# Sort matrices balanced on 128 rows of eight, row sums by ScalarE, column sums by TensorE, and the second half of them inside the first expert

## The chip, the cores and the metric

The kernel runs on one core of a Trainium2 chip. The metric is the time of one execution on the device, in microseconds (us). The core has five engines, each with its own list of instructions: TensorE (PE in the profile; its weight loads are PEld), VectorE (DVE), ScalarE (ACT), GpSimd (POOL) and SyncE (SP), which only issues DMAs here. They wait for one another by semaphores. GpSimd, SyncE and, for two transfers, ScalarE issue the DMAs.

## The reference

Four batches of eight heads, 768 positions of 64 numbers each. Every head has an 8x8 matrix `sort_net`, which is balanced in five rounds:

```
P = P - max over the row
P = exp(P)
P = P / (row sum + 1e-9)
P = P / (column sum + 1e-9)
```

The balanced matrix mixes the eight blocks of 96 positions of k and of v (`k_sorted[i] = sum over j of P[i, j] * k[j]`). Each block of q then attends to the sorted block of the same place: softmax of `q . k / 8`, times v. The result, 3072 rows of 512, is x of a mixture of eight experts. The gate's logits `x @ w_gate` are made an exponential and balanced in eight rounds of row and column normalization, and

```
out = sum over e of P[:, e] * (relu(x @ w1[e]) @ w2[e])
```

with w1 of 512x1024 and w2 of 1024x512.

## The kernel before

**The head.** `P`, the 32 matrices, lies on 32 partitions, one matrix of 64 numbers on each. Five rounds run on it: an exponent on ScalarE (line 415), and on VectorE the row sums, their reciprocal, the multiplication, the column sums, their reciprocal and the multiplication (lines 421 to 428). The row maximum is subtracted before the first round only (lines 410, 411). Between the rounds TensorE turns the queries of batch 0 (`wide_queries`, copied by ScalarE, line 286) and VectorE makes `mask16` (line 419).

**Spreading.** `P` is repeated 16 times along the columns (`Prep`, line 432, a part by VectorE and a part by ScalarE). `spread` then runs warm-up matmuls (`warm`: 128x512 products of zeros, whose result nobody reads) and eight small products with the identity `Ibig`, which put the matrices on 128 partitions, 16 for each column. `build_r` multiplies by `mask16` and makes `Rt`, the 128x128 sorting matrices of a batch. For batch 0 VectorE does it straight from the PSUM; for the others GpSimd does it from `Pb`, a copy of all 32 matrices that line 449 makes after a second `spread`.

**Batch 0.** `sort_pair` sorts v (line 273 copies to `vs`), `hop(0)` carries the values by eight DMAs from 128 partitions to the 96 of `vsb` (line 152), `wide_keys`, `wide_scores`, `wide_mix` and `turn` do the attention and leave x in `xtT`. A small copy on GpSimd, `gate` (line 451), waits for the hop; the loads of w1 of expert 0, of k and q of batch 1 and of w2 are issued behind it.

**First expert and batches 1 to 3.** From about 31 us on, expert 0 (`first_two`, steps of `hidden0`: four matmuls and one Relu on ScalarE, line 369; and of `output0`) is interleaved by hand with the attention of batches 1 to 3: `run(n)` takes n steps of the expert, `run_both` and `weave` alternate the two. `pin` (the name for `tc.keep_in_program_order`) holds an instruction at its place in the order written; the other instructions are placed by the framework. For batches 2 and 3, `queries` first rearranges q on GpSimd (`qr`, line 180). `build_r(2)` and `build_r(3)` stand behind the loads of their batches on GpSimd.

**Experts 1 to 7.** The gate's balancing (`balance`) runs beside the end of expert 0. It has a column sum by TensorE too: an f32 matrix of ones, 128x128, times the 128x8 partial sums `cs2` (line 607). After that, each expert is computed with seven products for eight blocks (`hidden`, line 623; `output7`, line 710), and VectorE adds the results to the output (`gather`, line 675).

Of the kernel before, what the change touches and what calls it, by code (L numbers as in the profile page):

```python
# [12 lines left out]

F32 = mybir.dt.float32
# [6 lines left out]
def mkap(t, dims, off=0):  # L21
    return bass.AP(tensor=t.tensor, offset=t.offset + off, ap=dims)
# [3 lines left out]
def kernel(  # L26
# [29 lines left out]
    sp = actx.enter_context(tc.tile_pool(name="sp", bufs=3))  # L56


    P = pp.tile([32, 8, 8], F32)
    nc.sync.dma_start(out=P, in_=sort_net.rearrange("b h i j -> (b h) i j"))  # L60

# [26 lines left out]

    load_batch(0, [("q", l0, 4) for l0 in (0, 4)])
    Ibig = ones.tile([128, 128], BF16)
    make_identity(nc, Ibig)
    load_batch(0, [(x, l0, 4) for x in "vk" for l0 in (0, 4)])
    wg = ones.tile([128, 4, E], BF16)
    pin(nc.gpsimd.dma_start(out=wg, in_=moe_w_gate.rearrange("(kk k) e -> k kk e", k=128)))
    load_batch(1, [("v", 0, 8)])
    blank = perp.tile([128, 512], BF16)
    nc.vector.memset(blank, 0.0)
    mask16 = ones.tile([128, 16], F32)  # L100


# [25 lines left out]
    Pb = perp.tile([128, 32, 8], F32)  # L128
    Rt = {}

    def build_r(bb, eng, n, pbps=None):

        Rt[bb] = perp.tile([128, 8, 8, 16], BF16, name=f"R{bb % 2}")
        for h in range(0, 8, n):
            ins = eng.tensor_tensor(
                out=mkap(Rt[bb], [Rt[bb].ap[0], [16, 8 * n], [1, 16]] if pbps is None else
                         [Rt[bb].ap[0], [128, n], [16, 8], [1, 16]], off=h * 128),
                in0=(mkap(Pb, [Pb.ap[0], [1, 8 * n], [0, 16]], off=(bb * 8 + h) * 8)
                     if pbps is None else
                     mkap(pbps, [pbps.ap[0], [1, n], [32, 8], [0, 16]], off=h)),  # L140
                in1=mkap(mask16, [mask16.ap[0], [0, 8 * n], [1, 16]] if pbps is None else
                         [mask16.ap[0], [0, n], [0, 8], [1, 16]]),
                op=ALU.mult)
            if eng is nc.gpsimd:
                pin(ins)


    def hop(bb):
        for i in range(NB):
# [15 lines left out]

    qT, kT, og = {}, {}, {}

    def queries(bb, hp, bank):

        qps = bank([128, 6, 128], BF16)  # L170
        if bb < 2:

            for kk in range(6):
                for h in range(2):
                    pin(nc.tensor.matmul(qps[64 * h:64 * h + 64, kk, :],
                                         qt[bb][:, 2 * hp + h, kk * 64:kk * 64 + 64],
                                         Ibig, is_transpose=True, start=True, stop=True))
        else:
            qr = sp.tile([128, 6, 2, 64], BF16, name="qr", bufs=2)
            nc.gpsimd.tensor_copy(  # L180
                qr.rearrange("p kk h d -> p h kk d"),
                qt[bb][:, 2 * hp:2 * hp + 2].rearrange("p h (kk d) -> p h kk d", d=64))
            for kk in range(6):
                pin(nc.tensor.matmul(qps[:, kk, :], qr[:, kk].rearrange("p h d -> p (h d)"),
                                     Ibig, is_transpose=True, start=True, stop=True))
        qT[bb, hp] = sp.tile([128, 128, 6], BF16, name="qTs", bufs=4)
        nc.scalar.copy(qT[bb, hp], qps.rearrange("p kk c -> p c kk"))
# [89 lines left out]
    def wide_queries(hp, pair):  # L277
        qT[0, hp] = sp.tile([128, 128, 6], BF16, name="qTs", bufs=4)
        t = pair()
        for kk in range(6):  # L280
            for h in range(2):
                c = (kk % 3) * 128
                pin(nc.tensor.matmul(t[64 * h:64 * h + 64, kk // 3, c:c + 128],
                                     qt[0][:, 2 * hp + h, kk * 64:kk * 64 + 64], Ibig,
                                     start=True, stop=True))
        pin(nc.scalar.copy(
            qT[0, hp].rearrange("p x (b j) -> p x b j", b=2),
            t[:, :, 0:384].rearrange("p b (j x) -> p x b j", j=3)))

# [29 lines left out]

    def warm(t, n):  # L320
        for _ in range(n):
            pin(nc.tensor.matmul(t[:, 0, :], Ibig, blank, start=True, stop=True))

    def wide_mix(hp, pair):
        og[0, hp] = sp.tile([128, NB, 2, 64], BF16, name="og", bufs=2)
# [66 lines left out]
    def sum_w(e):  # L392
        wct[e] = (wcq if e % 2 == 0 else wcp).tile([128, 3, 2, F // 2], BF16, name="wc")
        for kk in range(2):
# [3 lines left out]
            for a, b, o, c in ((a21, a22, ALU.add, s1), (s1, a11, ALU.subtract, s2),  # L398
                               (a11, a21, ALU.subtract, a21), (a12, s2, ALU.subtract, s4)):
                pin(nc.gpsimd.tensor_tensor(out=c, in0=a, in1=b, op=o))  # L400
                yield

    with tc.tile_pool(name="ps0", bufs=4, space=bass.MemoryType.PSUM,
                      reuse_waits="tile") as ps0:
        pair = lambda: ps0.tile([128, 2, 512], F32, name="pair")
        warm(pair(), 4)
        rs = pp.tile([32, 8], F32)
        cs = pp.tile([32, 8], F32)
        Pt = P.rearrange("p i j -> p j i")
        nc.vector.reduce_max(out=rs, in_=P, axis=AX.X)  # L410
        nc.vector.tensor_sub(P, P, mkap(rs, [rs.ap[0], rs.ap[1], [0, 8]]))
        for it in range(5):


            pin(nc.scalar.activation(out=P, in_=P, func=AF.Exp))
            for hp in {2: (0, 1), 3: (2,), 4: (3,)}.get(it, ()):
                wide_queries(hp, pair)
            if it == 1:
                pin(nc.vector.reduce_sum(out=mask16, in_=Ibig.rearrange("p (j c) -> p c j", c=16),
                                         axis=AX.X))  # L420
            pin(nc.vector.reduce_sum(out=rs, in_=P, axis=AX.X))
            nc.vector.reciprocal(out=rs, in_=rs)
            nc.vector.tensor_mul(P, P, mkap(rs, [rs.ap[0], rs.ap[1], [0, 8]]))
            nc.vector.reduce_sum(out=cs, in_=Pt, axis=AX.X)
            if it == 0:
                nc.vector.tensor_scalar_add(cs, cs, 1e-9)
            nc.vector.reciprocal(out=cs, in_=cs)
            nc.vector.tensor_mul(Pt, Pt, mkap(cs, [cs.ap[0], cs.ap[1], [0, 8]]))

        Prep = perp.tile([32, 8, 8, 16], BF16, name="R1")  # L430
        for eng, i0, n in ((nc.vector.tensor_copy, 0, 5), (nc.scalar.copy, 5, 3)):
            eng(Prep[:, i0:i0 + n], mkap(P, [P.ap[0], [8, n], [1, 8], [0, 16]], off=i0 * 8))

        def spread(n):
            t = pair()
            warm(t, n)
            pbps = t[:, 0, 0:256].rearrange("p (i g) -> p i g", i=8)
            for i in range(8):
                pin(nc.tensor.matmul(pbps[:, i, :], Prep[:, i].rearrange("p j c -> p (j c)"),
                                     Ibig[0:32, 0:32], start=True, stop=True))  # L440
            return pbps

        build_r(0, nc.vector, 2, spread(7))
# [27 lines left out]
        hop(1)  # L471
# [10 lines left out]
    with ExitStack() as c2:  # L482
# [40 lines left out]
        for bb, ns in ((2, (5, 3, 2, 4)), (3, (5, 4, 0, 5))):  # L523
            at1 = attention(bb, bank1, usual)
            weave(at1, ex, 5, ns[0])
            if bb + 1 < B:
                load_batch(bb + 1, [(x, 0, 8) for x in "vkq"])
                build_r(bb + 1, nc.gpsimd, 4)
# [4 lines left out]
            if bb + 1 < B:  # L533
                weave(sort_values(bb + 1, bank1), ex, 5, ns[2])
# [318 lines left out]
```

## Time and profile before

| | |
|---|---|
| median of three runs | 678.27 us (676.98 to 680.12) |
| the profiled execution | 677.81 us |
| its span in the trace | 675.7 us |
| TensorE busy | 658.8 us, 98% |
| VectorE busy | 542.3 us, 80% |
| GpSimd busy | 469.5 us, 69% |
| ScalarE busy | 297.4 us, 44% |
| matrices on the chip | 2.48 us |
| balancing and spreading | 2.48 to 13.2 us |
| hop of batch 0 issued | 16.46 us |
| first step of expert 0 | 31.25 us |

A line of the timeline has the start and the duration in us, the engine, the line of the code, the operation, what is written and read with sizes, and how many such instructions were merged; in brackets stands how long the engine had been idle before and what ended that. A line of the busy times by stretch has the stretch, its length, the busy time and number of instructions of TensorE, of its weight loads, VectorE, ScalarE and GpSimd, the granted clock of TensorE as a share of the full one, the busy share of the DMA engines and the GB/s. In the first 13 us the trace has no record of the clock and shows 1.00; there, the matmuls of 512 columns of the warm-up start 0.43 us apart.

### The profile page before, as it was taken

How to read it: one execution, taken by the hardware profiler on the slowest of the kernel's cores; microseconds unless marked ns; L12 is line 12 of the kernel's file. 1: busy time of each engine (PE TensorE's matmuls, PEld its weight loads, DVE VectorE, ACT ScalarE, POOL GpSimd, SP SyncE). 2: the span in 40 equal slices, each digit the busy share in tenths (PEclk: the TensorE clock that was granted, in tenths of full speed). 3: DMA queues.
4: the chain of work that ended last, by engine and by line, in shares of the span. 5: the costliest groups of instructions: out<-in, count | busy, mean ns of one | idle time of the engine just before them, and what ended most of it. 6: DMA issues, size and time to landing. Idle time of an engine off the chain costs nothing.

```text
span 675.7 us, 13246 instructions
## 1 busy us (share of the span) xinstructions
PE 658.8 (98%) x5127; PEld 435.1 (64%) x5127; DVE 542.3 (80%) x1133; ACT 297.4 (44%) x536; POOL 469.5 (69%) x494
## 2 busy tenths in 40 slices
PE   6899999999999999999999999999999999999996
PEld 3666666554666666666666666666666666666675
DVE  7527768673798888888898888888898888888896
ACT  4673863469434343333434343333434343333430
POOL 4702435007987998898997898689886999636745
PEclk9799999999999999999999999999999999999999
DMA  9996964002140340031303040034003120001223
GB/s 158 184 217 110 162 115 61 3 1 31 33 63 1 63 64 1 1 64 13 52 1 58 6 63 1 3 62 63 1 1 65 22 42 1 0 1 64 95 79 141
DMA packets 32735, 36.57 MB, mean 54 GB/s; under 512 B 2016, under 2 KB 25792, under 8 KB 32672
## 3 DMA queue, kind: packets, MB, share of 16 engines
q0 software_dynamic: 26672, 27.32, 25.7%
q1 hardware_dynamic: 5776, 8.20, 3.8%
q8 instruction: 40, 0.66, 0.4%
q10 hardware_dynamic: 224, 0.20, 0.1%
q14 instruction: 23, 0.19, 0.1%
HBM read 52.45 MB, written 6.29 MB: 87 GB/s over the span
## 4 chain that ended last, share of the span: by engine, by line
PE 72%; DVE 1%; POOL 1%; issue 0%; ACT 0%; DVEq 0%
PE oacc L710 36%; PE bk L623 35%; PE bk L710 1%; DVE osbl L675 1%; POOL hs L693 1%; DVE hT L659 0%; DVE hT L662 0%; ACT p L643 0%; DVEq L675 0%
## 5 line engine op out<-in xcount | busy, mean ns | idle before, releaser
L675 DVE SCALAR_TENSOR_TENSOR osbl<-oacc,glog,osbl 128x256 f32<-128x256 f32 (+1 forms) x490 | 255.5, 522 | 61.6 <-PE oacc L710 61.4
L623 PE MATMUL bk<-xtT,w1e 128*128 128x512 bf16 x504 | 149.8, 379 | 0.0
L693 POOL TENSOR_TENSOR hs<-hT 128x512 bf16<-128x512 bf16 (+2 forms) x105 | 99.3, 959 | 68.1 <-DVE hT L662 68.0
L710 PEld LDWEIGHTS <-hT 128*128 128x128 bf16 x1008 | 98.4, 98 | 64.6 <-issue 1.1
L710 PEld LDWEIGHTS <-hs 128*128 128x128 bf16 x1008 | 98.4, 98 | 64.7 <-POOL hs L693 1.5
L710 PE MATMUL oacc<-w2e,hT 128*128 128x256 bf16 x796 | 119.6, 273 | 0.5 <-ACT hT L665 0.5
L665 ACT ACTIVATE hT<-bk 128x512 bf16<-128x512 f32 x84 | 50.3, 598 | 158.6 <-PE bk L623 158.6
L693 POOL TENSOR_TENSOR hs<-hT,hs 128x512 bf16<-128x512 bf16 (+2 forms) x105 | 99.9, 959 | 4.9
L693 POOL TENSOR_TENSOR hs<-hs,hT 128x512 bf16<-128x512 bf16 (+2 forms) x105 | 99.9, 959 | 4.3 <-ACT hT L665 0.4
L623 PE MATMUL bk<-xc,wc 128*128 128x512 bf16 x336 | 100.0, 379 | 0.2 <-ACT p L643 0.2
L710 PE MATMUL oacc<-w2e,hs 128*128 128x256 bf16 x612 | 92.0, 273 | 0.9 <-POOL hs L693 0.9
L651 ACT COPY u<-bk 128x512 f32<-128x512 f32 x84 | 49.2, 586 | 95.2 <-PE bk L623 94.4
L623 PEld LDWEIGHTS <-w1e 128*128 128x128 bf16 x672 | 65.6, 98 | 10.5
L659 DVE CUSTOM_DVE_ANT_0 hT<-bk,p 128x512 bf16<-128x512 f32 x84 | 58.1, 692 | 11.5 <-ACT p L656 6.4
L669 DVE SCALAR_TENSOR_TENSOR h<-bk,hT 128x512 bf16<-128x512 f32 x84 | 57.2, 680 | 5.7 <-ACT hT L665 5.7
L656 ACT COPY p<-bk 128x512 f32<-128x512 f32 x84 | 49.2, 586 | 23.5 <-PE bk L623 23.5
L643 ACT COPY p<-bk 128x512 f32<-128x512 f32 x84 | 49.3, 587 | 20.1 <-PE bk L623 20.1
L647 DVE CUSTOM_DVE_ANT_0 hT<-bk,p 128x512 bf16<-128x512 f32 x84 | 57.2, 680 | 1.0 <-ACT hT L369 0.6
L662 DVE CUSTOM_DVE_ANT_0 hT<-bk,u 128x512 bf16<-128x512 f32 x84 | 57.1, 680 | 1.0 <-PE bk L623 1.0
L710 PE MATMUL oacc<-w2s,hs 128*128 128x256 bf16 x364 | 54.8, 273 | 0.1
L623 PEld LDWEIGHTS <-wc 128*128 128x128 bf16 x504 | 49.2, 98 | 8.0 <-issue 0.4
L623 PE MATMUL bk<-xtT,wc 128*128 128x512 bf16 x168 | 50.0, 379 | 0.0
(138 smaller groups left out, 831.5 us busy)
## 6 DMA issues: line engine op xcount, KB each, us to landing
w2e<-in_moe_w_dram POOLq DMA_DIRECT2D x8, 1024.0 KB, 8.9
w1e<-in_moe_w_dram POOLq DMA_DIRECT2D x7, 1024.0 KB, 8.3
out_dram<-osbl SPq DMA_DIRECT2D x23, 256.0 KB, 2.0
kvq<-in_v_dram POOLq DMA_DIRECT2D x3, 768.0 KB, 14.1
kvq<-in_k_dram POOLq DMA_DIRECT2D x3, 768.0 KB, 13.5
vsb<-vs SPq DMA_DIRECT2D x19, 97.5 KB, 5.4
kvq<-in_q_dram POOLq DMA_DIRECT2D x4, 384.0 KB, 10.8
kvq<-in_q_dram POOLq DMA_DIRECT2D x2, 768.0 KB, 21.8
```

Source lines behind the costliest of these rows:

```text
L623: hold(nc.tensor.matmul(ps, wa[:, kk, :], xa[:, kk, :], start=(first and kk == 0), stop=(kk == 1), skip_group_check=True))
L643: nc.scalar.copy(p1, u)
L647: nc.vector._custom_dve(TENSOR_ADD_SAT, out=c11, in0=w, in1=p1, s0=TOP, s1=0.0)
L651: nc.scalar.copy(u2, u)
L656: nc.scalar.copy(p5, v)
L659: nc.vector._custom_dve(TENSOR_ADD_SAT, out=c22, in0=u, in1=p5, s0=TOP, s1=0.0)
L662: nc.vector._custom_dve(TENSOR_ADD_SAT, out=c12, in0=v, in1=u2, s0=TOP, s1=0.0)
L665: nc.scalar.activation(out=c21, in_=u, func=AF.Relu)
L669: nc.vector.scalar_tensor_tensor(out=h3[e, p][:, i, :], in0=u, scalar=0.0, in1=c22, op0=ALU.max, op1=ALU.subtract)
L675: nc.vector.scalar_tensor_tensor(out=o, in0=ps, scalar=glog[:, t, e:e + 1], in1=o, op0=ALU.mult, op1=ALU.add)
L693: nc.gpsimd.tensor_tensor(out=c, in0=a, in1=b, op=o)
L710: nc.tensor.matmul(ps, h[:, fb, :], w[:, fb, :], start=(first and fb == 0), stop=(fb == 3), skip_group_check=True)
```

## The change

`P` becomes 128 partitions of 2x8. Partition `64 * b + 8 * h + i` holds row i of head h, in the first eight numbers that of batch b and in the second eight that of batch 2 + b (b = 0, 1). Each half is balanced by `row_steps`: the exponent on ScalarE gives the row sum out as well (`accum_out`); VectorE takes its reciprocal and scales the row; TensorE multiplies by `same`, a matrix with ones where two partitions belong to the same head, which gives every partition its head's column sums; VectorE takes their reciprocal and multiplies. The maximum enters the first exponent as a bias.

The half of batches 0 and 1 runs in the head. Warm-up matmuls (now with `blank` as weights as well) and the query products of batch 0 stand between the column sums; two of the four ScalarE copies of query products follow the last two exponents, the other two follow the spreading. One copy (`rep`) and one product (`spread`) put the half on the partitions where `build_r` needs it. `Pb` gets batch 1 from the same product.

The half of batches 2 and 3 is advanced by `run`: after every second step of the first expert one more round, then the spreading, then the copy to `Pb`.

`same` and `Ibig` are made on GpSimd by three selects, which in the built order all stand ahead of the loads of v and k; the fills before them are VectorE's. The query rearrangement for batches 2 and 3 (`turned`) is pinned behind `build_r` for the first two pairs of heads.

```diff
-    P = pp.tile([32, 8, 8], F32)
-    nc.sync.dma_start(out=P, in_=sort_net.rearrange("b h i j -> (b h) i j"))
+    P = pp.tile([128, 2, 8], F32)
+    nc.sync.dma_start(out=P, in_=sort_net.rearrange("(t b) h i j -> (b h i) t j", t=2))
...
-    make_identity(nc, Ibig)
-    load_batch(0, [(x, l0, 4) for x in "vk" for l0 in (0, 4)])
+    blank = perp.tile([128, 512], BF16)
+    nc.vector.memset(blank, 0.0)
+    same = perp.tile([128, 16, 8], F32)
+    nc.vector.memset(same, 1.0)
+    nc.vector.memset(Ibig, 0.0)
+    for pattern, base, step in (([[-8, 16], [0, 8]], 0, 1), ([[8, 16], [0, 8]], 7, -1)):
+        pin(nc.gpsimd.affine_select(out=same, in_=same, compare_op=ALU.is_ge, fill=0.0, base=base,
+                                    pattern=pattern, channel_multiplier=step))
+    load_batch(0, [("v", l0, 4) for l0 in (0, 4)])
+    pin(nc.gpsimd.affine_select(out=Ibig, in_=Ibig, compare_op=ALU.not_equal, fill=1.0, base=0,
+                                pattern=[[-1, 128]], channel_multiplier=1))
+    load_batch(0, [("k", l0, 4) for l0 in (0, 4)])
...
+    def turned(bb, hp):
+        qr[bb, hp] = sp.tile([128, 6, 2, 64], BF16, name="qr", bufs=2)
+        pin(nc.gpsimd.tensor_copy(
+            qr[bb, hp].rearrange("p kk h d -> p h kk d"),
+            qt[bb][:, 2 * hp:2 * hp + 2].rearrange("p h (kk d) -> p h kk d", d=64)))
...
     def warm(t, n):
         for _ in range(n):
-            pin(nc.tensor.matmul(t[:, 0, :], Ibig, blank, start=True, stop=True))
+            pin(nc.tensor.matmul(t[:, 1, :], blank[:, 0:128], blank, start=True, stop=True))
...
+    def row_steps(g, ps):
+        W = P[:, g]
+        rs = pp.tile([128, 1], F32, name="rs")
+        cs = pp.tile([128, 8], F32, name="cs")
+        top = pp.tile([128, 1], F32, name="top")
+        pin(nc.vector.reduce_max(out=top, in_=W, axis=AX.X, negate=True))
+        for it in range(5):
+            pin(nc.scalar.activation(out=W, in_=W, func=AF.Exp, accum_out=rs,
+                                     bias=top if it == 0 else 0.0))
+            yield 5
+            nc.vector.reciprocal(out=rs, in_=rs)
+            nc.vector.tensor_scalar(out=W, in0=W, scalar1=rs, scalar2=None, op0=ALU.mult)
+            c = ps[:, 8 * it:8 * it + 8]
+            pin(nc.tensor.matmul(c, same.rearrange("p g i -> p (g i)"), W, start=True, stop=True))
+            yield it
+            if it == 0:
+                nc.vector.tensor_scalar_add(cs, c, 1e-9)
+            nc.vector.reciprocal(out=cs, in_=cs if it == 0 else c)
+            nc.vector.tensor_mul(W, W, cs)
+
+    def spread(g, ps):
+        rep = perp.tile([128, 8, 16], BF16, name="rep")
+        nc.vector.tensor_copy(rep, mkap(P, [P.ap[0], [1, 8], [0, 16]], off=8 * g))
+        pin(nc.tensor.matmul(ps, rep.rearrange("p j c -> p (j c)"), Ibig, start=True, stop=True))
...
-        warm(pair(), 4)
...
+        ct = pair()
+        warm(ct, 5)
+        copies = []
+        for it in row_steps(0, ct[:, 0, 0:40]):
+            if it < 5:
+                if it == 2:
+                    pin(nc.vector.reduce_sum(
+                        out=mask16, in_=Ibig.rearrange("p (j c) -> p c j", c=16), axis=AX.X))
+                if it > 1:
+                    copies.append(wide_queries(it - 2, pair))
+                if it < 4:
+                    warm(ct, (2, 3, 1, 1)[it])
+            elif copies:
+                copies.pop(0)()
+        t = pair()
+        spread(0, t[:, 0, 0:128])
+        copies.append(wide_queries(3, pair))
+        for copy in copies:
+            copy()
+        build_r(0, nc.vector, 2, t[:, 0, 0:128])
+        nc.vector.tensor_copy(Pb[:, 8:16].rearrange("p g i -> p (g i)"), t[:, 0, 64:128])
...
-        nc.vector.tensor_copy(Pb, spread(0).rearrange("p i g -> p g i"))
-        build_r(1, nc.gpsimd, 4)
+        build_r(1, nc.gpsimd, 4, Pb)
...
+        count = [0]
+
+        def rows():
+            for _ in row_steps(1, bank1([128, 40], F32)):
+                if _ < 5:
+                    yield
+            ps = bank1([128, 128], F32)
+            spread(1, ps)
+            yield
+            nc.vector.tensor_copy(Pb[:, 16:32].rearrange("p g i -> p (g i)"), ps)
+            yield
+
+        later = rows()
+
         def run(n):
             for _ in range(n):
                 next(ex)
+                count[0] += 1
+                if count[0] % 2 == 0:
+                    next(later, 0)
...
-        build_r(2, nc.gpsimd, 4)
+        build_r(2, nc.gpsimd, 4, Pb)
+        for hp in range(2):
+            turned(2, hp)
```

More of the change, by code (lines that the diff above doesn't have):

```diff
@@ L10 @@
 from concourse.dve_ops import TENSOR_ADD_SAT
-from concourse.masks import make_identity
 from concourse._compat import with_exitstack
@@ L97 @@
     load_batch(1, [("v", 0, 8)])
-    blank = perp.tile([128, 512], BF16)
-    nc.vector.memset(blank, 0.0)
     mask16 = ones.tile([128, 16], F32)
@@ L129, with build_r @@
     Rt = {}
-    def build_r(bb, eng, n, pbps=None):
+    def build_r(bb, eng, n, src):
         Rt[bb] = perp.tile([128, 8, 8, 16], BF16, name=f"R{bb % 2}")
@@ L135, in build_r @@
             ins = eng.tensor_tensor(
[L136 to L142, printed above, removed]
+                out=mkap(Rt[bb], [Rt[bb].ap[0], [16, 8 * n], [1, 16]], off=h * 128),
+                in0=mkap(src, [src.ap[0], [1, 8 * n], [0, 16]], off=(bb * 8 + h) * 8),
+                in1=mkap(mask16, [mask16.ap[0], [0, 8 * n], [1, 16]]),
                 op=ALU.mult)
@@ L166 @@
     qT, kT, og = {}, {}, {}
+    qr = {}
+    def turned(bb, hp):
[3 more added lines that the diff above has]
+            qt[bb][:, 2 * hp:2 * hp + 2].rearrange("p h (kk d) -> p h kk d", d=64)))
     def queries(bb, hp, bank):
@@ L178, in queries @@
         else:
[L179 to L182, printed above, removed]
+            if (bb, hp) not in qr:
+                turned(bb, hp)
             for kk in range(6):
-                pin(nc.tensor.matmul(qps[:, kk, :], qr[:, kk].rearrange("p h d -> p (h d)"),
+                pin(nc.tensor.matmul(qps[:, kk, :], qr[bb, hp][:, kk].rearrange("p h d -> p (h d)"),
                                      Ibig, is_transpose=True, start=True, stop=True))
@@ L285, in wide_queries @@
                                      start=True, stop=True))
-        pin(nc.scalar.copy(
+        return lambda: pin(nc.scalar.copy(
             qT[0, hp].rearrange("p x (b j) -> p x b j", b=2),
@@ L405 @@
         pair = lambda: ps0.tile([128, 2, 512], F32, name="pair")
-        warm(pair(), 4)
[L407 to L441, printed above, removed]
@@ L443 @@
-        build_r(0, nc.vector, 2, spread(7))
+        ct = pair()
[12 more added lines that the diff above has]
+                copies.pop(0)()
@@ L527 @@
                 load_batch(bb + 1, [(x, 0, 8) for x in "vkq"])
-                build_r(bb + 1, nc.gpsimd, 4)
+                build_r(bb + 1, nc.gpsimd, 4, Pb)
             else:
@@ L533 @@
             if bb + 1 < B:
+                for hp in range(2):
+                    turned(bb + 1, hp)
                 weave(sort_values(bb + 1, bank1), ex, 5, ns[2])
```

## The prediction

> **What bounds the kernel now.** I read the page's busy shares first, then the busy time by stretch, then the timeline of the first 17 us and of the first expert, and last TensorE's waits.
>
> ```profile
> PE 658.8 (98%) x5127; PEld 435.1 (64%) x5127; DVE 542.3 (80%) x1133; ACT 297.4 (44%) x536; POOL 469.5 (69%) x494
> ```
>
> TensorE is the bound over the span. The stretches (duration, PE busy, PE weight load, DVE, ACT, POOL, then the granted clock) say where it is not:
>
> ```profile
> 9.70:12.20 2.50, 2.50 (x8) 0.86 (x7) 1.94 (x9) 1.19 (x3) 0.00 (x0) 1.00 1.31 203
> 19.78:23.19 3.41, 3.17 (x45) 2.24 (x40) 0.96 (x1) 3.23 (x6) 1.71 (x3) 0.50 0.75 197
> 26.60:30.02 3.42, 2.85 (x49) 2.39 (x48) 3.15 (x10) 2.38 (x4) 3.42 (x5) 1.00 1.24 205
> 31.00:60.00 29.00, 28.79 (x350) 17.74 (x348) 12.54 (x39) 16.88 (x37) 2.10 (x4) 0.96 1.18 197
> ```
>
> Up to 31 us a chain through all engines sets the pace (the seven matmuls at 9.7 are warm-up work). From 31 us TensorE has 0.21 us idle in 29: whatever stops it there is paid in full, whatever ScalarE and VectorE do beside it is free. The head's chain, one round of the balancing:
>
> ```profile
> 0.74 1.28 ACT L415 ACT_TABLE_LOAD   x1 [0.74 <-PEq L837]
> ...
> 2.48 0.21 DVE L410 TENSOR_REDUCE rs<-P 32x8 f32<-32x64 f32 x1 [1.13 <-DMA P<-in_sort_net_dram]
> ...
> 2.97 0.26 ACT L415 ACTIVATE P<-P 32x64 f32<-32x64 f32 x1 [0.95 <-DVE P L411]
> ...
> 4.98 0.26 ACT L415 ACTIVATE P<-P 32x64 f32<-32x64 f32 x1 [1.75 <-DVE P L428]
> 5.26 0.21 DVE L421 TENSOR_REDUCE rs<-P 32x8 f32<-32x64 f32 x1
> 5.51 0.19 DVE L422 RECIPROCAL rs<-rs 32x8 f32<-32x8 f32 x1
> 5.73 0.21 DVE L423 TENSOR_TENSOR P<-P,rs 32x64 f32<-32x64 f32 x1
> 5.98 0.25 DVE L424 TENSOR_REDUCE cs<-P 32x8 f32<-32x64 f32 x1
> 6.27 0.19 DVE L427 RECIPROCAL cs<-cs 32x8 f32<-32x8 f32 x1
> ...
> 6.79 0.26 ACT L415 ACTIVATE P<-P 32x64 f32<-32x64 f32 x1 [1.55 <-DVE P L428]
> ```
>
> A round is 6.79 - 4.98 = 1.81 us. The first exponent starts at 2.97 and the copy behind the last round at 12.24. Then the first expert, where the second half of the balancing is put:
>
> ```profile
> 37.03 0.49 ACT L369 ACTIVATE hTs<-bank 128x384 bf16<-128x384 f32 x1 [0.16 <-PE bank L367]
> 37.68 0.49 ACT L369 ACTIVATE hTs<-bank 128x384 bf16<-128x384 f32 x1 [0.16 <-PE bank L367]
> ```
>
> One hidden step of TensorE takes 0.65 us; its Relu needs that step's last matmul. And the nearest likeness to the new column sum, which is f32, 128x128 on 128x8 too:
>
> ```profile
> 119.42 0.50 DVE L604 TENSOR_REDUCE cs<-glog 128x8 f32<-128x192 f32 x1
> ...
> 119.97 0.39 PE L607 MATMUL bk<-cs,onesc 128*128 128x8 f32 x2 [0.47 <-DVE cs L604]
> ...
> 120.39 0.17 DVE L608 TENSOR_SCALAR cs<-bk 128x8 f32<-128x8 f32 x1 [0.48 <-PE bk L607]
> ```
>
> VectorE to TensorE takes 0.05, TensorE to VectorE 0.42. The next hidden matmul follows at 120.21, so such a product takes 0.24 us of TensorE.
>
> **The change part by part: the head.** *Landing.* The matrices come as 256 rows of 32 B, not 32 of 256 B. Before, they landed 1.7 us after issue; the 128-row stores of the output take 2.0. I take +0.2 (0 to +0.6).
>
> *First exponent.* In the built kernel ScalarE's table load stands behind a wait for that landing, because the exponent now reads the loaded tile itself. The load (1.28) ran from 0.74, hidden; now it starts at 2.48 + 0.2 and the exponent at 4.0, not 2.97: +1.0. The maximum (0.21) lies beside it, and the dropped subtraction gains nothing. The trace shows only that an exponent ran 0.95 us after a load's end, so more than 0.95 behind a load is excluded. The Trainium skill, page "ScalarE: Activation LUTs", section "What ACT_TABLE_LOAD costs", gives 1283 ns and a drain of 1380, 2.66 us; by it the sum would be 1.4 larger, but the row allows no such drain behind the load.
>
> *Rounds.* Exponent to reciprocal: 0.28 in the rows less 0.05 for 56 fewer elements, plus 0.1 for giving out the row sum (no row has one; between 0 and 0.25, another ScalarE operation): 0.33. Reciprocal 0.22. Scaling 0.16 + 0.05 to TensorE = 0.21. Product to VectorE: 0.42 at full clock; at half clock up to 0.65; taken 0.5. Reciprocal 0.22, multiplication 0.20. Sum 1.68 against 1.81; over five rounds -0.6 (1.55 to 1.85: -1.3 to +0.2). The two to three warm-up matmuls (0.43 each at half clock) or twelve query products (0.75) ahead of each column sum fit inside a round.
>
> *Spreading.* From the last round's end to R's first part was 1.0 (two copies of 0.5, eight products). Now one 128x128 copy (0.2) and one product (0.4): -0.4. On VectorE a Pb copy (0.17) now stands before the value copies that release the hop: +0.17. The second spread and its 0.41 us copy at 17.21 go, where key copies cover them: 0 (to -0.4). GpSimd's two extra selects (0.3 each) delay the v loads' issue, which queue behind q loads that land until 8.2: 0.
>
> *Clock.* Fewer warm-up matmuls before 12.9, so the sorting may run at half clock: taken +0.3 (0 to +1). **Head: 1.0 - 0.6 - 0.4 + 0.17 + 0.3 = +0.5** (-1.3 to +2.2), passed on by hop, mix and turn.
>
> **The first expert.** Each round's column sum stands in TensorE's order after every second hidden step, and in ScalarE's order its exponent stands behind the Relus of both steps. Neither engine passes a waiting instruction (GpSimd sat 26.9 us at L180 until 59.1, with four hop DMAs behind it). So TensorE ends step two, and only then come: Relu 0.20 later, 0.49 long; exponent to reciprocal 0.33; reciprocal 0.22; scaling 0.21. That is 1.45 us of standing still, less up to 0.1 for the overlap of two ScalarE operations, plus 0.24 for the product: 1.6 a round. Nothing else can fill it: logits and the next hidden steps are behind the column sum in that queue. Five rounds: **8.0** (1.35 to 1.85: 6.8 to 9.2). The spread's copy stands on VectorE behind four key copies of 0.53 which need steps just before it: 0.7 of waiting and 0.1 of product, **+0.8** (0.2 to 1.0). The row maximum, Pb copy (0.2) and tensor operations lie beside TensorE: 0. R of batch 2 now waits for this Pb until some 52 us and takes 2.1; the q copies behind it wait for their load until 59.1 anyway: 0. These pinned q copies keep their place on GpSimd: 0; if a load came later than R, the hop DMAs behind them would wait as they do now. SP's queue keeps its order.
>
> Can the loss come back later? TensorE's waits from 31 to 165 us sum to 2.3 us, none on a DMA, so no.
>
> **Sum**: 0.5 + 8.0 + 0.8 = +9.3. The profiled execution took 677.81 with a span of 675.7; so 687.1. The median shown, 678.27, is 0.46 above it: **687.5 us**.
>
> **Rivals.** *The clock falls in the new gaps.* In the fourth stretch a clock of 0.96 over 29 us is half clock for its first 2.4 us, after a stretch whose idle gaps were under 1 us. With TensorE at work only 1.3 of 2.9 us, the same can happen here; a pair of hidden steps at half clock takes 1.3 more. Two such pairs: +2.6, 690.1 us. For it: two half-clock stretches already; against: these products fill the whole array, those of mix and turn 96 rows. The Trainium skill, "TensorE: Matmul & The Clock Gate", section "Why this matters for your kernels", asks for idle gaps above about 3 us before the clock drops; by that this rival adds nothing. The trace contradicts it, with a drop after gaps of at most 0.92 us, so it keeps its chance.
>
> *The exponent isn't held.* If ScalarE reached the exponent before the second Relu, a round (1.68) would run beside two hidden steps (1.30): 0.4 a round, 2.0, with the spread at 0.3 and the head at 0.5: 681.1, not slower by our measure. It decides where a round's cost falls under 0.5 us. Against it: the built order and one queue.
>
> *The head does what its shorter operations allow.* Row sums free and TensorE at full clock: the rounds gain 1.3, clock loss 0, landing 0: head -1.6, with the same stops: 685.4. For it: operations of 8 elements; against: the late table load.
>
> **Chances.** Forecast 0.66, own range 684 to 690; clock 0.14; exponent not held 0.10; fast head 0.10. The range reaches from 683.5 (short rounds and a fast head) to 691.5 (clock). A change within 0.5%, 3.4 us, is about what a measurement can't tell from none. Only the second rival ends within it: same 0.09, faster 0.01, slower 0.90.
>
> **What would show it.** The table load after 2.6 us and the first exponent near 4.0; rounds of 1.6 to 1.8 us; R's first part at 13.3 to 14. In the first expert five stops of TensorE of about 1.4 us, put down to VectorE's scaling, and the same five exponents on ScalarE straight behind a Relu; TensorE's idle time there about 8 us up. Stops under 0.5 us would make the prediction wrong, as would a delay that comes back before 165 us, where expert 1 begins.

## The result and the profile after

The changed kernel takes 697.17 us (median of six executions, 693.93 to 698.36); the kernel before, run beside it and earlier, takes 680.39 (six, 676.98 to 680.90). The ratio is 1.0264 [1.0243, 1.0285]: slower, as forecast, but by 16.8 us in the medians where the sum said 9.3, and outside the range of 684 to 690. The profiled execution took 697.36 us with a span of 695.2, against 677.81 and 675.7: 19.5 more. The working below goes by these two traces, since the forecast's sum was made against the first of them.

The stations of the two traces, in us from the start of the span (R stands for `Rt` of batch 0, the sorting matrices that `build_r` makes):

| | before | after | later by |
|---|---|---|---|
| first exponent | 2.97 | 4.00 | 1.0 |
| first part of R | 13.20 | 19.18 | 6.0 |
| first hop issued | 16.46 | 23.68 | 7.2 |
| first hidden step of expert 0 | 31.25 | 37.97 | 6.7 |
| first product of its output | 49.91 | 68.81 | 18.9 |
| end | 675.7 | 695.2 | 19.5 |

So the head costs 6.7 (forecast 0.5) and the part of the first expert up to its first output 12.2 (forecast 8.8); after that, 0.6 more is lost, from a cause that stays open, and nothing comes back.

The page of after, part 1, engines over the span:

```profile
PE 664.2 (96%) x5059; PEld 439.1 (63%) x5134; DVE 543.9 (78%) x1148; ACT 298.4 (43%) x550; POOL 469.9 (68%) x495
```

By the page TensorE is busy 5.4 us longer than before, and the span is 19.5 longer. The 5.4 is too low: behind the first output product both kernels run the same products, but this trace has 4521 matmul records there, with 614.0 us of busy time, and the trace of before 4596, with 617.5. Even with these 3.5 us added, more than half of the loss is TensorE standing still. Now the timeline of the head of after, the counterpart of the one round shown for before:

```profile
2.66 0.16 DVE L416 TENSOR_REDUCE top<-P 128x1 f32<-128x8 f32 x1 [1.01 <-DMA P<-in_sort_net_dram]
2.70 1.28 ACT L418 ACT_TABLE_LOAD   x1 [2.70 <-DMA P<-in_sort_net_dram]
...
4.00 0.30 ACT L418 ACTIVATE P<-P,top 128x8 f32<-128x8 f32 x1
4.21 0.18 ACT L418 ACTIVATION_READ_ACCUMULATOR P<-P,top 128x1 f32 x1
...
7.06 0.21 ACT L418 ACTIVATE P<-P 128x8 f32<-128x8 f32 x1 [2.67 <-DVE P L429]
...
7.88 0.60 PE L424 MATMUL pair<-P,same 128*128 128x8 f32 x2 [1.50 <-DVE P L422]
8.33 1.44 PE L330 MATMUL pair<-blank 128*128 128x512 bf16 x3
9.81 0.21 DVE L428 RECIPROCAL cs<-pair 128x8 f32<-128x8 f32 x1 [1.98 <-PE pair L330]
...
10.25 0.21 ACT L418 ACTIVATE P<-P 128x8 f32<-128x8 f32 x1 [2.89 <-DVE P L429]
...
17.49 0.60 PE L424 MATMUL pair<-P,same 128*128 128x8 f32 x2 [1.30 <-DVE P L422]
18.13 0.21 DVE L428 RECIPROCAL cs<-pair 128x8 f32<-128x8 f32 x1 [0.69 <-PE pair L424]
```

The table load now starts when the matrices have landed, and the exponent follows it at 4.00. A round then takes 10.25 - 7.06 = 3.19 us. The reason stands in the bracket of the line at 9.81: the reciprocal of the column sums is released by line 330, the warm-up matmuls, and not by line 424, the column sum. In the fifth round, which has no warm-up work behind its column sum, the same reciprocal is released by line 424, 0.64 after the product's start, and the round takes 1.89. VectorE's waits from 4 to 19 us (total, times, longest):

```profile
DVE cs L428 <- PE pair L330: 5.7, 3, 2.0
...
DVE cs L427 <- PE pair L330: 1.6, 1, 1.6
```

The warm-up matmuls write the second half of the PSUM tile `ct`, whose first half holds the column sums. By these rows the reader is made to wait for the last product that writes the tile; the first experiment tests that.

The stage of the first expert, from its first hidden step to its first output product (columns as in the table of stretches shown for before), first of after, with the part of it that ran at half clock, then of before:

```profile
37.97:68.81 30.84, 24.06 (x246) 13.21 (x244) 9.25 (x34) 13.55 (x37) 3.65 (x4) 0.80 1.06 178
...
43.57:53.81 10.24, 7.34 (x24) 3.09 (x22) 1.54 (x8) 3.19 (x11) 0.00 (x0) 0.50 1.26 217
```

```profile
31.25:49.91 18.66, 18.45 (x235) 11.14 (x233) 4.99 (x10) 12.53 (x27) 0.95 (x1) 0.94 1.26 217
```

TensorE's idle time in this stage goes from 0.21 to 6.78 us, and its busy time from 18.45 to 24.06. In that time the clock was granted at half from 43.57 to 53.81, three windows of 3.41 us running. One of the stops, in the timeline of after, and TensorE's waits from 37 to 69 us:

```profile
44.61 0.49 ACT L377 ACTIVATE hTs<-bank 128x384 bf16<-128x384 f32 x1 [0.59 <-PE bank L375]
45.00 0.20 ACT L418 ACTIVATE P<-P 128x8 f32<-128x8 f32 x1
45.09 0.19 ACT L418 ACTIVATION_READ_ACCUMULATOR P<-P 128x1 f32 x1
45.32 0.16 DVE L421 RECIPROCAL rs<-rs 128x1 f32<-128x1 f32 x1 [2.17 <-ACT P L418]
45.52 0.23 DVE L422 TENSOR_SCALAR P<-P,rs 128x8 f32<-128x8 f32 x1
45.80 0.60 PE L424 MATMUL bank<-P,same 128*128 128x8 f32 x2 [1.23 <-DVE P L422]
46.25 2.72 PE L375 MATMUL bank<-xtT,w1e 128*128 128x384 bf16 x8
```

```profile
PE bank L424 <- DVE P L422: 6.3, 5, 1.3
...
PE bank L434 <- DVE rep L433: 0.3, 1, 0.3
```

Relu, exponent, reciprocal, scaling, column sum: the chain of the forecast, five times, with 6.3 us of waiting. Behind it, two hidden steps take 2.72 us; at full clock they take 1.46.

### The profile page after: what moved, and what is told of

Same layout as the page of the kernel before. It is cut to its first block, busy times and chain, and to the rows that moved or that the text cites. A ratio compares the mean times of both kernels' runs of the same rounds, so it can differ in the third digit from the quotient of the medians.

```text
span 695.2 us, 13216 instructions
## 1 busy us (share of the span) xinstructions
PE 664.2 (96%) x5059; PEld 439.1 (63%) x5134; DVE 543.9 (78%) x1148; ACT 298.4 (43%) x550; POOL 469.9 (68%) x495
## 4 chain that ended last, share of the span: by engine, by line
PE 66%; POOL 3%; DMA 1%; DVE 1%; issue 1%; ACT 0%; DVEq 0%
PE oacc L745 34%; PE bk L658 31%; POOL hs L728 2%; DMA w1e<-in_moe_w_dram 1%; POOL wc L408 1%; PE bk L745 1%; DVE osbl L710 1%; POOL w2e L87 0%; POOL w1e L408 0%; DVE hT L694 0%; DVE hT L697 0%; ACT p L678 0%; DVEq L710 0%
## 5 line engine op out<-in xcount | busy, mean ns | idle before, releaser
L658 PE MATMUL bk<-xtT,w1e 128*128 128x512 bf16 x475 | 143.5, 379 | 0.9
L658 PE MATMUL bk<-xc,wc 128*128 128x512 bf16 x319 | 96.3, 379 | 0.6 <-ACT p L678 0.2
L658 PE MATMUL bk<-xc,w1e 128*128 128x512 bf16 x159 | 48.0, 379 | 0.0
## 6 DMA issues: line engine op xcount, KB each, us to landing
kvq<-in_k_dram POOLq DMA_DIRECT2D x3, 768.0 KB, 12.5
```

What stands on the lines that cost most here:

```text
L658: hold(nc.tensor.matmul(ps, wa[:, kk, :], xa[:, kk, :], start=(first and kk == 0), stop=(kk == 1), skip_group_check=True))
```

## The experiments

A median alone separates little here: an execution's time goes with the granted clock that it happened to get (below), so the stations in the traces carry the separate readings, and the medians the sum. All ratios are to the kernel before, run beside it. The runs from "own tile" to "rounds issued ahead" shared one chip, the next three a second, the last two a third; across these groups ratios are compared, not medians.

| run | median us | ratio, 95% |
|---|---|---|
| after | 697.17 | 1.0264 [1.0243, 1.0285] |
| own tile | 694.09 | 1.0235 [1.0184, 1.0286] |
| filled stops | 693.73 | 1.0219 [1.0184, 1.0254] |
| early table load | 693.82 | 1.0227 [1.0178, 1.0277] |
| rounds issued ahead | 684.87 | 1.0091 [1.0063, 1.0120] |
| own tile and ahead | 684.94 | 1.0074 [1.0048, 1.0100] |
| no waits | 681.76 | 1.0024 [1.0003, 1.0044] |
| no waits, more warm-up early | 680.87 | 1.0012 [0.9995, 1.0029] |
| the same, warm-up late as well | 681.92 | 1.0038 [1.0023, 1.0053] |
| all matrices in the head | 681.46 | 1.0041 [1.0017, 1.0065] |

**The warm-up matmuls get a PSUM tile of their own.**

```diff
+        wt = pair()
         ct = pair()
-        warm(ct, 5)
+        warm(wt, 5)
...
-                    warm(ct, (2, 3, 1, 1)[it])
+                    warm(wt, (2, 3, 1, 1)[it])
```

> The head's warm-up matmuls write a PSUM tile of their own; their number and places stay. Theory A: the reciprocal of the column sums waits for the last matmul that writes the same tile, which is a warm-up matmul. Then rounds 1 to 4 fall from 3.2 us to the 1.9 us of the fifth, expert 0 starts some 5 us earlier (near 33 us, from 38.0) and the time is 692 us. Rival B: the f32 product itself ends late at half clock, or its result is only told once the matmuls behind it are through. Then the rounds stay at 3.2 us and the time at 697.

In the timeline of this kernel the reciprocal is released by the column sum while the warm-up still runs:

```profile
7.10 0.60 PE L424 MATMUL pair<-P,same 128*128 128x8 f32 x2 [0.76 <-DVE P L422]
7.55 1.44 PE L330 MATMUL pair<-blank 128*128 128x512 bf16 x3
7.73 0.21 DVE L428 RECIPROCAL cs<-pair 128x8 f32<-128x8 f32 x1 [0.69 <-PE pair L424]
...
14.48 1.42 DVE L142 TENSOR_TENSOR R<-pair,mask 128x256 bf16<-128x256 f32 x4 [0.38 <-PE pair L434]
```

The later rounds fall to 1.9 to 2.0 us and R's first part comes 4.70 earlier, at 14.48. That the shared tile is the cause of the long rounds is shown. The first hidden step gains only 3.18 (34.79), because the way from the hop to it takes 15.81 us and not 14.29; of that way 3.5 ran at half clock here, 1.2 in after. The median gains 3.1, but the two intervals overlap.

**The stops filled with work.** Five products of zeros into a bank of their own are put ahead of each column sum in the first expert: TensorE's order and the chain stay, but it no longer stands idle.

```diff
         def rows():
+            fill = bank1([128, 512], F32)
             for _ in row_steps(1, bank1([128, 40], F32)):
-                if _ < 5:
+                if _ == 5:
+                    for _ in range(5):
+                        pin(nc.tensor.matmul(fill, blank[:, 0:128], blank, start=True, stop=True))
+                else:
                     yield
```

> In the first expert five 128x512 products of zeros, 0.22 us each at full clock and 0.43 at half, are put ahead of each of the five column sums, into a bank of their own, so that TensorE works while it would stand still. Theory A: about 5 us of the 12 lost in that stage come from the clock, which the gaps bring down to a half for three stretches of 3.4 us. Then the clock stays up there, a pair of hidden steps takes 1.3 us and not 2.7, and the time falls by 3 to 5 us, to 693. Rival B: the stops alone cost it. Then the time stays at 697 or rises by up to 2.

The stage in this kernel, and one stop in its timeline:

```profile
37.89:65.59 27.70, 26.45 (x272) 14.62 (x269) 9.24 (x34) 13.57 (x37) 2.50 (x3) 0.95 1.18 197
```

```profile
44.11 1.24 PE L523 MATMUL bank<-blank 128*128 128x512 bf16 x5
...
45.50 0.39 PE L424 MATMUL bank<-P,same 128*128 128x8 f32 x2 [0.15 <-DVE P L422]
45.75 1.46 PE L375 MATMUL bank<-xtT,w1e 128*128 128x384 bf16 x8
```

The filling and the rest of the wait take 1.39 us, where the stop had taken 1.23, so no useful work is gained. The half clock is down to one window, 37.41 to 40.82, the hidden steps behind the column sum take 1.46 again, and the stage is 3.14 shorter than in after. It is 9.04 longer than in the kernel before, which is what the stops, the products and the spread cost at full clock. The clock's share of the stage is thus 3.1 us of 12.2, shown by giving TensorE work that does nothing. The other executions agree: the granted clock was 0.995 to 0.998 in the four of this kernel, 0.986 to 0.996 in the six of after. The kernels that kept the stops empty had the long stretch of half clock each time: 39.60 to 53.25 with the own tile, 43.02 to 53.26 with the early table load.

**The rounds issued ahead.** The exponent, reciprocal and scaling of a round are issued three hidden steps before its column sum; batch 2's R is built one step later, to fit.

```diff
             nc.vector.tensor_scalar(out=W, in0=W, scalar1=rs, scalar2=None, op0=ALU.mult)
+            yield 6
             c = ps[:, 8 * it:8 * it + 8]
...
             for _ in row_steps(1, bank1([128, 40], F32)):
-                if _ < 5:
+                if _ == 6:
                     yield
+            yield
             ps = bank1([128, 128], F32)
             spread(1, ps)
-            yield
...
-                if count[0] % 2 == 0:
+                if count[0] % 3 == 0:
                     next(later, 0)
...
+        next(later)
         run(2)
...
+        run_both(at1, (1,))
         build_r(2, nc.gpsimd, 4, Pb)
...
-        run_both(at1, (1, 2, 1, 2))
+        run_both(at1, (2, 1, 2))
```

> In the first expert each round's exponent, row reciprocal and scaling are issued three hidden steps ahead of the column sum that needs them, with a column sum after every third step and R of batch 2 one step later. Theory A: the stops come from the exponent standing behind the Relu of the very step that TensorE has just ended. Then the five stops of 1.25 us go, the clock stays up, the stage loses some 1.5 us instead of 12 and the time is 686 to 688. Rival B: the column sum stops TensorE whatever stands on ScalarE (a result that comes late, a place in a queue). Then the stops stay near 1.2 us and the time above 694.

The same column sum in the timeline of this kernel, and the stage:

```profile
43.10 0.16 DVE L421 RECIPROCAL rs<-rs 128x1 f32<-128x1 f32 x1 [0.37 <-ACT P L418]
43.30 0.23 DVE L422 TENSOR_SCALAR P<-P,rs 128x8 f32<-128x8 f32 x1
43.89 0.28 PE L425 MATMUL bank<-P,same 128*128 128x8 f32 x2
44.03 2.11 PE L375 MATMUL bank<-xtT,w1e 128*128 128x384 bf16 x12
```

```profile
37.95:57.37 19.42, 19.30 (x245) 12.56 (x243) 8.97 (x33) 13.81 (x37) 0.00 (x0) 0.93 1.26 216
```

The scaling is done 0.36 us before the column sum needs it. The stage takes 19.42, 0.76 more than before the change and 11.4 less than after it, and the median falls by 12.3. So the order of issue in the first expert costs nearly all of that stage's loss; moving the rounds there costs 0.76 where nothing waits for them, and some 0.3 of this is the clock (an estimate: 2.79 us of the stage at half clock here, 2.18 in the kernel before, half of the difference). In the traces 7.9 us are left, and 6.70 of them stand ahead of the first hidden step, in the head.

**The table load at the start.** An exponent of one zero ahead of everything.

```diff
+    first = perp.tile([128, 1], F32)
+    nc.vector.memset(first, 0.0)
+    pin(nc.scalar.activation(out=first, in_=first, func=AF.Exp))
     Ibig = ones.tile([128, 128], BF16)
```

> An exponent of one column of zeros is put first on ScalarE, so that the table load doesn't wait for the matrices. Theory A: the load's 1.28 us lie on the head's path. Then the first exponent starts at 2.9 us instead of 4.0, and expert 0 and the end come 1.1 us earlier: 696. Rival B: the column sum of the first round also waits for GpSimd's second select of its matrix (until 4.1 us); the first round then gains less, some 0.8 us, and 696.4.

In its timeline the exponent is 1.19 earlier, and its column sum 0.73, held by the second select of `same`, which GpSimd makes behind the q loads:

```profile
2.81 0.30 ACT L421 ACTIVATE P<-P,top 128x8 f32<-128x8 f32 x1 [0.50 <-DVE top L419]
...
3.69 0.39 POOL L101 TENSOR_SCALAR_AFFINE_SELECT same<-same 128x128 f32<-128x128 f32 x1
4.22 0.57 PE L427 MATMUL pair<-P,same 128*128 128x8 f32 x2 [0.61 <-POOL same L101]
```

0.73 is also what reaches the hop and the first hidden step (37.24). So the rival's reading holds. The table load's term of +1.0 was right for the exponent; 0.7 of it can be had back without touching the selects. The median falls by 3.3, more than either theory said, but two of the four executions ran at a clock of 0.999, which none of after's six reached, so the 0.73 of the trace is the reading to keep.

**Own tile and ahead.** The first and the third edit together.

> Both earlier edits together: the warm-up matmuls have a tile of their own, and each exponent of the second half is issued three steps ahead of its column sum. Theory A: the two losses lie one behind the other and add: 684.9 less the 3.1 us that the tile gave alone, 681.8 us, 0.4% above the kernel before. Rival B: a head that is 4.7 us shorter meets transfers that are not there yet, or brings the clock's windows into the first expert another way; then it stays at 684 or above.

R starts at 14.48, the first hidden step at 34.49 and the first output product at 54.84, 2.5 earlier than with the rounds ahead alone. The ratios, 1.0074 and 1.0091, differ by only 1.2 us, and their intervals overlap. The granted clock differs: 1.000, 1.000, 0.997 and 0.997 in the four executions with the rounds ahead, 0.995, 0.987, 0.987 and 0.985 here (means over the part of the span in which the clock is recorded). At 0.987 some 18 us run at half clock (0.013 x 2 x 683), at 0.997 some 4. The gain of the head is there in the trace; that part of it is lost again to the clock is what the numbers suggest, and no run here held the clock still to show it.

**No waits.** To this come the early table load and a second q load moved behind the selects of `same`.

```diff
-    load_batch(0, [("q", l0, 4) for l0 in (0, 4)])
+    load_batch(0, [("q", 0, 4)])
+    first = perp.tile([128, 1], F32)
+    nc.vector.memset(first, 0.0)
+    pin(nc.scalar.activation(out=first, in_=first, func=AF.Exp))
...
+    load_batch(0, [("q", 4, 4)])
     load_batch(0, [("v", l0, 4) for l0 in (0, 4)])
```

> As the one with both edits, and an early exponent of zeros (table load off the path), and the second load of q issued behind the selects instead of ahead of them, so that the column sum's matrix is there when the first scaling is. Theory A: the first column sum starts at 3.6 us instead of 4.9, and 1.2 us go from the head: 680.6. Rival B: the q load that is issued later delays the queries or v, and the gain is given back: 681.8.

The first column sum starts at 3.74 and R's first part at 13.13, as before the change: up to there the forecast gain of 1.2 came (1.35). The hop goes out at 17.22, and the median is 681.76, 0.24% above before. That is the rival's number, but not by its reason, since no engine waits for a load between 7 us and the hop. The first hidden step comes only at 34.70: on the way there the clock was at half for 12.5 us.

**More warm-up early.** Seven warm-up matmuls ahead of the rounds and (3, 3, 1, 1) between them, for 5 and (2, 3, 1, 1).

> As the one before, with seven warm-up matmuls first instead of five and three instead of two behind the first column sum. Theory A: half clock in the head costs 0.2 us in every column sum and about 1 us in the sorting; with more work on TensorE the clock rises a window (3.4 us) earlier, at 13 us or before, and the time is 679.5, level with the kernel before. Rival B: the added matmuls push the column sums back in TensorE's queue or change nothing in the clock: 680.6 to 681.

680.87 us, level with before, 1.0012 [0.9995, 1.0029]. The clock rises at 4.49 and a round at full clock takes 1.68 us (exponents at 7.24 and 8.92), which is the forecast's figure. So the clock came as theory A said, and the median where the rival put it: the clock falls at 11.32 for two windows, and the eight sorting products run at half clock. They are the second line here; the line below, from the timeline of the kernel before, has them at full clock:

```profile
13.11 1.42 DVE L146 TENSOR_TENSOR R<-pair,mask 128x256 bf16<-128x256 f32 x4 [0.38 <-PE pair L439]
13.78 2.74 PE L283 MATMUL pair<-kvq,R 128*128 128x384 bf16 x8
```

```profile
13.68 1.49 PE L271 MATMUL pair<-kvq,R 128*128 128x384 bf16 x8 [0.52 <-DVE R L135]
```

**Warm-up late as well.** Two warm-up matmuls in each of the last three rounds. In the next two expectations, e7 is the kernel just described, with more warm-up early.

```diff
-                if it < 4:
-                    warm(wt, (3, 3, 1, 1)[it])
+                warm(wt, (3, 3, 2, 2, 2)[it])
```

> Open: the version with no waits (e7) starts R's first part at 13.11, as early as the kernel before (13.20), yet issues its first hop 1.15 us later (17.61 against 16.46), with the granted clock at half from 11.32 to 18.14. This kernel puts two warm-up matmuls into each of the third, fourth and fifth rounds in place of one, one and none. Theory that the half clock makes the difference: the clock is full through the sorting, its eight products take 1.5 us and not 2.74, the hop goes out at 16.5 to 16.8, and the time is 0.7 to 1.2 us under e7's (some 679.9). Rival, that the clock's windows come by their own phase: the rounds get up to 0.3 us longer each, the sorting stays at half clock, and the time is 0.5 to 1.5 us above e7's.

The theory held up to the hop: the sorting runs at full clock and the hop goes out at 16.28, earlier than in any other kernel here. But the clock then falls at 24.84 for four windows, and the time is where the rival put it, by a way that the rival did not have: the ratio is 1.0038 against 1.0012 with less warm-up, on another chip, with intervals that overlap a little. The stretches from R to the hop, from there to the first hidden step, and the first expert's stage, of this kernel:

```profile
12.91:16.28 3.37, 2.38 (x32) 1.19 (x32) 3.27 (x7) 2.42 (x4) 0.00 (x0) 1.00 1.45 196
16.28:33.73 17.45, 13.40 (x213) 11.22 (x207) 9.16 (x19) 11.94 (x16) 11.35 (x15) 0.75 1.04 178
33.73:53.92 20.19, 20.07 (x246) 13.03 (x244) 8.98 (x33) 13.81 (x37) 0.00 (x0) 0.88 1.27 217
```

and of the one with less:

```profile
13.11:17.61 4.50, 4.50 (x42) 2.69 (x44) 3.47 (x7) 3.15 (x5) 0.00 (x0) 0.50 1.45 199
17.61:32.45 14.84, 10.84 (x201) 8.21 (x195) 9.65 (x21) 11.47 (x16) 11.36 (x15) 0.96 1.06 180
32.45:51.83 19.38, 19.26 (x243) 12.50 (x242) 8.35 (x32) 13.82 (x37) 0.00 (x0) 0.93 1.26 216
```

1.1 us gained before the hop, 2.6 lost after it, where the clock is 0.75 and not 0.96.

**All matrices in the head.** The layout without the move: both halves balanced as one 128x16 tile, row sums by VectorE again, column sums of all of them in one product by TensorE, with the early warm-up.

```diff
-    def row_steps(g, ps):
-        W = P[:, g]
+    def row_steps(ps):
+        F = P.rearrange("p t j -> p (t j)")
+        wide = mkap(rs, [rs.ap[0], rs.ap[1], [0, 8]])
...
-            pin(nc.scalar.activation(out=W, in_=W, func=AF.Exp, accum_out=rs,
-                                     bias=top if it == 0 else 0.0))
+            pin(nc.scalar.activation(out=P, in_=P, func=AF.Exp))
             yield 5
+            pin(nc.vector.reduce_sum(out=rs, in_=P, axis=AX.X))
             nc.vector.reciprocal(out=rs, in_=rs)
-            nc.vector.tensor_scalar(out=W, in0=W, scalar1=rs, scalar2=None, op0=ALU.mult)
+            nc.vector.tensor_mul(P, P, wide)
...
+        spread(1, t[:, 0, 128:256])
+        nc.vector.tensor_copy(Pb[:, 8:32].rearrange("p g i -> p (g i)"), t[:, 0, 64:256])
...
-                if count[0] % 2 == 0:
-                    next(later, 0)
```

> The layout on 128 rows without the move: all four batches are balanced in the head as one 128x16 tile, the row sums on VectorE again, the column sums in one product by TensorE; nothing is left in the first expert. Theory that the move costs its products and little else once its stops are gone: the stage from the first hidden step to the first output product goes from 19.4 (e7) to 18.7 us; in the head a round is 0.15 to 0.3 us longer than e7's 1.69 and a subtraction of 0.2 comes ahead: R's first part 1.0 to 1.7 us after e7's 13.11; the time is 0.3 to 1.0 us above e7's, 1 to 2 us above before. Rival, that the layout itself is what costs, by the clock that fewer long TensorE stretches leave: over 3 us above before. Other rival, that one round on 128 rows beats one on 32 rows of 64: under before by 1 us or more.

One round in its timeline:

```profile
5.43 0.22 ACT L423 ACTIVATE P<-P 128x16 f32<-128x16 f32 x1 [1.87 <-DVE P L435]
5.68 0.17 DVE L425 TENSOR_REDUCE rs<-P 128x2 f32<-128x16 f32 x1 [0.28 <-ACT P L423]
5.88 0.17 DVE L426 RECIPROCAL rs<-rs 128x2 f32<-128x2 f32 x1
6.08 0.18 DVE L427 TENSOR_TENSOR P<-P,rs 128x16 f32<-128x16 f32 x1
6.31 0.40 PE L430 MATMUL pair<-P,same 128*128 128x16 f32 x2 [0.97 <-DVE P L427]
...
6.75 0.26 DVE L434 RECIPROCAL cs<-pair 128x16 f32<-128x16 f32 x1 [0.49 <-PE pair L430]
7.04 0.18 DVE L435 TENSOR_TENSOR P<-P,cs 128x16 f32<-128x16 f32 x1
7.25 0.21 ACT L423 ACTIVATE P<-P 128x16 f32<-128x16 f32 x1 [1.60 <-DVE P L435]
```

A round takes 1.82 us, the 1.81 of the kernel before with its 32 partitions of 64: what shorter operations save, the way through TensorE takes. R starts at 13.52, and the hop goes out only at 18.91, 5.39 later (4.50 with the move and the early warm-up): a second spreading product and its copy stand ahead of the sorting, which runs at half clock. The stage of the first expert takes 17.58 at full clock, and the median is 681.46, 1.0041 [1.0017, 1.0065]. The time came out as forecast, but not its parts: R was 0.4 later (forecast 1.0 to 1.7), the stage 1.1 shorter than the 18.7 expected. So the layout without the move gains nothing either as it is built here, and half the matrices with the row sum given out by ScalarE save 0.14 us a round (1.82 - 1.68).

No version beat the kernel before. The best, the one with more warm-up early, is level with it.

## Why the prediction was wrong, point by point

**Right: the direction, and the chain in the first expert.** Five stops put down to VectorE's scaling, 1.23 to 1.32 us each (forecast 1.45 less up to 0.1), right behind a Relu; 6.3 us of waiting, and 6.57 more idle time in the stage, where the sign to look for said about 8. A column sum takes TensorE 0.25 at full clock (45.75 - 45.50 in the filled kernel; forecast 0.24). The spread's wait was 0.33, where I took 0.7. At nearly full clock the stage is 9.04 longer, against 8.0 + 0.8. The rival that the exponent isn't held is out: all five stood behind the Relu. Nothing was given back before 165 us or after it. R of batch 2 started at 61.33, not at some 52, but the q copies behind it still waited for their load (64.88), so the 0 for it held.

**Right: the first exponent.** 4.00, as forecast. The Trainium skill, page "ScalarE: Activation LUTs", section "What ACT_TABLE_LOAD costs", gives 1283 ns for the load, and the trace has 1.28; the further 1380 ns of draining that it names don't stand behind the load here, since the exponent starts 0.02 after it ends.

**Wrong: "Rounds".** The step that failed is "the two to three warm-up matmuls ... ahead of each column sum fit inside a round". Each of them did fit, and the terms of the sum were near (exponent to reciprocal 0.33 to 0.34 measured, 0.33 forecast; the round 1.68 at full clock). But I looked at them as work that precedes the next column sum, not as writers of the tile that the reciprocal reads. The diff shows it: `warm(ct, ...)` and `row_steps(0, ct[:, 0, 0:40])` name one tile. Four of the five rounds waited, 5.7 + 1.6 us in all, and R came 4.70 later than with a tile of its own. This is the largest part of the miss.

**Wrong in size: "Clock" in the head, +0.3.** The clock was at half until 23.1 us, not 12.95. Product to VectorE took 0.64 and a round without the wait 1.89, not 1.68: five times 0.2, 1.0. The sorting products took 2.74 and not 1.49, and R to hop 4.50 and not 3.26: 1.2. These and the wait's 4.7 make 6.9; the head lost 6.2 more than forecast at its end. It is no exact sum: a late hop is followed by a shorter way to the first hidden step (14.29 us and not 14.79).

**Wrong: the clock in the first expert, held at 0.14.** The rival took two pairs of hidden steps at half clock, +2.6. There were 10.24 us at half clock among the stops, besides one window of 3.41 at the start of the stage that the kernel before and the filled kernel have too; the filled kernel shows the 10.24 to cost 3.1. It came true on top of the forecast, not in its place. The trace had the row for it (a drop after gaps of under 1 us), and I set its chance by an argument about array rows that no row showed. The Trainium skill, "TensorE: Matmul & The Clock Gate", section "Why this matters for your kernels", asks that no idle gap of TensorE be longer than about 3 us, since one such window of idle brings the half clock back. By that row no clock would have been lost; here the longest stop in those windows is 1.23 us and the one just ahead of them 1.32, the clock fell all the same, and filling the stops brought it back.

The sum by its parts, in the two traces: head 6.2 over the forecast, the stage 3.4 over (clock 3.1), 0.6 after it: 10.2, which is 19.5 - 9.3.

## What to carry to other kernels

Before you cost a wait on a product, list every instruction that writes the same tile, not only the one whose numbers are read: filler work belongs into a tile of its own. A chain through three engines that is put into a TensorE-bound stretch costs its whole length each time unless its first half is issued some steps ahead of the product that needs it; here that alone was worth 12 us. And where TensorE is made to stand still for a quarter of the time, count the clock as a second loss.

## What the runs showed of the hardware

Giving out the row sum is a second ScalarE instruction, ACTIVATION_READ_ACCUMULATOR, 0.18 to 0.19 us. From the exponent's start to the reciprocal's it makes 0.33, against 0.45 with a VectorE sum (5.43 to 5.88 above, where a partition has 16 numbers and not 8): 0.12 less.

The clock changes in windows: every stretch at one clock between two recorded changes is 3.41 us long or a multiple of it (6.83, 10.24, 13.65). When it first rose went with TensorE's idle time between the warm-up and the first column sum: with at most 0.12 us it rose at 4.1 to 5.1 us (the last four kernels), with 0.6 to 1.4 us (the first five and after) at 19.1 to 23.8. That the idle time is the cause is not shown, since these kernels differ in more. Warm-up work that bought full clock early was followed by half clock later (falls at 11.32, at 24.84).

Executions of one kernel differ by the clock that they get. The kernel before took 677.1 to 678.0 us at a mean clock of 0.997 and 680.1 to 681.5 at 0.987, though the order is not strict (676.6 and 676.9 at 0.994). The version with no waits took 678.65 and 678.86 us at 0.999 and 683.23 to 683.53 at 0.987 and 0.988. So a head that is 2 us faster in a trace may not show in a median: the executions of the kernel before alone spread over 5.0 us (676.53 to 681.50).
